# Transposing x by DMA on its way in, with a written issue order, in a one-core SwiGLU kernel

## The chip, the cores and the metric

The kernel runs on one core of one Trainium2 chip. The metric is device time in microseconds (us), median of several runs. The profile also gives a span, from the first to the last instruction; in every run listed with a span the time is about 1.8 us longer than the span. With one core there is no second core to compare with, so a run is called slow when it is over 1.5% above the fastest run of the same kernel, and fast otherwise.

Words used below: TensorE does the matmuls and writes them to PSUM (the tiles gate_ps, up_ps, o_ps and pT); VectorE and ScalarE do the elementwise work; SyncE's queue issues the DMA transfers, so a transfer has an issue (the queue is occupied; 0.44 us for the first load of x in the kernel before) and a landing (the data has arrived; 3.5 us after the start of that issue). The warm-up is a row of matmuls without use, run while the first data is on its way, meant to have TensorE's clock up when real work begins: in the kernel before the warm-up's matmuls run 427 ns apart, those of the steady stretches 216. In the profile lines PE is TensorE, PEld its weight loads, DVE VectorE, ACT ScalarE, POOL GpSimd and SPq SyncE's queue; PE, PEclk and DMA rows have one digit per fortieth of the span (a slice, counted from 0): busy tenths, or tenths of the full clock.

## The reference

```python
B, S, D, F = 32, 32, 512, 1792        # bf16; B*S = 1024 rows
gate = x @ w1                          # [1024, 512] x [512, 1792]
up   = x @ w3
h    = silu(gate) * up
out  = h @ w2                          # [1024, 1792] x [1792, 512]
```

In this kernel both operands of a matmul lie with the dimension that is summed over on the 128 partitions (the rows of on-chip memory), so the projections need x with its 512 columns on partitions, that is transposed.

## The kernel before

x is loaded as it lies (two loads of 512 KB), transposed on TensorE in 128x128 tiles through PSUM, and copied to `xT`. The Tile scheduler decides the order of each engine's instructions.

```python
nc.sync.dma_start(out=x_sb[:, 0:half, :], in_=x_view[:, 0:half, :])
for i, (cb0, cb1) in enumerate(bounds):            # chunks of 2, 2, 2, 4, 4 tiles of F
    nc.sync.dma_start(out=w1_sb[...], in_=w1_v[...])
    nc.sync.dma_start(out=w3_sb[...], in_=w3_v[...])
    if i == 3:
        nc.sync.dma_start(out=x_sb[:, half:NT, :], in_=x_view[:, half:NT, :])
# ... w2 in two halves, nine warm-up matmuls on a zeroed tile ...
def x_transposes(nb):
    for dt in range(DT):
        pT = psum_t.tile([P, NB], bf16, name="pT", tag="tp")
        for j in range(NT_PER_BLK):
            nt = nb * NT_PER_BLK + j
            nc.tensor.transpose(pT[:, j*P:(j+1)*P], x_sb[:, nt, dt*P:(dt+1)*P], ident[:])
        # copy pT to xT: VectorE for block 0, ScalarE for block 1
for nb in range(NBLK):                              # 2 blocks of 512 rows
    x_transposes(nb)
    for fo in range(FT):                            # 14 tiles of F
        # 4 gate matmuls, 4 up matmuls (128x512), sigmoid, two multiplies into hT
# then 8 tiles of out: 14 matmuls each over hT and w2, copy, store
```

Of the kernel before, what the change touches and what calls it, by code (L numbers as in the profile page):

```python
# [1 line left out]

# [5 lines left out]


@with_exitstack
def kernel(
    ctx: ExitStack,
    tc: tile.TileContext,
    x: bass.AP,
    w1: bass.AP,
    w3: bass.AP,
    w2: bass.AP,
    out: bass.AP,
):  # L20
    nc = tc.nc
    P = nc.NUM_PARTITIONS
    fp32 = mybir.dt.float32
    bf16 = mybir.dt.bfloat16

    B, S, D = x.shape
    F = w1.shape[1]
    N = B * S
    assert D % P == 0 and F % P == 0 and N % P == 0
    DT = D // P  # L30
    FT = F // P
    NT = N // P
    NB = 512
    assert N % NB == 0 and NB % P == 0
    NBLK = N // NB
    NT_PER_BLK = NB // P

    x_flat = x.flatten_outer_dims()
    out_flat = out.flatten_outer_dims()
    x_view = x_flat.rearrange("(nt p) d -> p nt d", p=P)  # L40
    w1_v = w1.rearrange("(dt p) f -> p dt f", p=P)
    w3_v = w3.rearrange("(dt p) f -> p dt f", p=P)
    w2_v = w2.rearrange("(ft p) d -> p ft d", p=P)

    consts = ctx.enter_context(tc.tile_pool(name="consts", bufs=1))
    work = ctx.enter_context(tc.tile_pool(name="work", bufs=3))
    psum_t = ctx.enter_context(tc.tile_pool(name="psum_t", bufs=2, space=bass.MemoryType.PSUM))
    psum = ctx.enter_context(tc.tile_pool(name="psum", bufs=2, space=bass.MemoryType.PSUM))
    psum2 = ctx.enter_context(tc.tile_pool(name="psum2", bufs=2, space=bass.MemoryType.PSUM))

    warm_sb = consts.tile([P, NB], bf16, name="warm_sb")
    nc.gpsimd.memset(warm_sb[:], 0.0)  # L52
    ident = consts.tile([P, P], bf16, name="ident")
    make_identity(nc, ident[:])

    x_sb = consts.tile([P, NT, D], bf16, name="x_sb")
    xT = consts.tile([P, DT, N], bf16, name="xT")
    w1_sb = consts.tile([P, DT, F], bf16, name="w1_sb")
    w3_sb = consts.tile([P, DT, F], bf16, name="w3_sb")
    w2_sb = consts.tile([P, FT, D], bf16, name="w2_sb")  # L60
    hT = consts.tile([P, FT, N], bf16, name="hT")

    half = NT // 2
    nc.sync.dma_start(out=x_sb[:, 0:half, :], in_=x_view[:, 0:half, :])  # L64

    chunk_sizes = [2, 2, 2, 4, 4]
    bounds = []
    cb = 0
    for csz in chunk_sizes:
        ce = min(FT, cb + csz)  # L70
        if cb < ce:
            bounds.append((cb, ce))
        cb = ce
    assert cb >= FT, (cb, FT)

    for i, (cb0, cb1) in enumerate(bounds):
        f0, f1 = cb0 * P, cb1 * P
        nc.sync.dma_start(out=w1_sb[:, :, f0:f1], in_=w1_v[:, :, f0:f1])  # L78
        nc.sync.dma_start(out=w3_sb[:, :, f0:f1], in_=w3_v[:, :, f0:f1])  # L79
        if i == 3:  # L80
            nc.sync.dma_start(out=x_sb[:, half:NT, :], in_=x_view[:, half:NT, :])

    FH = FT // 2
    nc.sync.dma_start(out=w2_sb[:, 0:FH, :], in_=w2_v[:, 0:FH, :])
    nc.sync.dma_start(out=w2_sb[:, FH:FT, :], in_=w2_v[:, FH:FT, :])

    NWARM = 9
    warm_ps = psum_t.tile([P, NB], fp32, name="warm_ps", tag="tp")
    for i in range(NWARM):
        nc.tensor.matmul(  # L90
            warm_ps[:],
            lhsT=warm_sb[:, 0:P],
            rhs=warm_sb[:],
            start=True,
            stop=True,
        )

    def x_transposes(nb: int):
        for dt in range(DT):
            pT = psum_t.tile([P, NB], bf16, name="pT", tag="tp")  # L100
            for j in range(NT_PER_BLK):
                nt = nb * NT_PER_BLK + j
                nc.tensor.transpose(  # L103
                    pT[:, j * P : (j + 1) * P],
                    x_sb[:, nt, dt * P : (dt + 1) * P],
                    ident[:],
                )
            if nb == 0:
                nc.vector.tensor_copy(xT[:, dt, nb * NB : (nb + 1) * NB], pT[:])  # L109
            else:  # L110
                nc.scalar.copy(xT[:, dt, nb * NB : (nb + 1) * NB], pT[:])  # L111

    for nb in range(NBLK):
        x_transposes(nb)
        for fo in range(FT):
            gate_ps = psum.tile([P, NB], fp32, name="gate_ps")
            up_ps = psum.tile([P, NB], fp32, name="up_ps")
            for dt in range(DT):
                nc.tensor.matmul(  # L119
                    gate_ps[:],  # L120
                    lhsT=w1_sb[:, dt, fo * P : (fo + 1) * P],
                    rhs=xT[:, dt, nb * NB : (nb + 1) * NB],
                    start=(dt == 0),
                    stop=(dt == DT - 1),
                )
            for dt in range(DT):
                nc.tensor.matmul(  # L127
                    up_ps[:],
                    lhsT=w3_sb[:, dt, fo * P : (fo + 1) * P],
                    rhs=xT[:, dt, nb * NB : (nb + 1) * NB],  # L130
                    start=(dt == 0),
                    stop=(dt == DT - 1),
                )
            sig = work.tile([P, NB], fp32, name="sig")
            nc.scalar.activation(  # L135
                sig[:], gate_ps[:], mybir.ActivationFunctionType.Sigmoid
            )
            t = work.tile([P, NB], fp32, name="t")
            nc.vector.tensor_mul(t[:], gate_ps[:], sig[:])  # L139
            nc.vector.tensor_mul(hT[:, fo, nb * NB : (nb + 1) * NB], t[:], up_ps[:])  # L140

    for nt in range(NT):
        DB = 256 if nt == NT - 1 else 512
        assert D % DB == 0
        for db in range(D // DB):
            o_ps = psum2.tile([P, DB], fp32, name="o_ps", tag="o_ps")
            for fo in range(FT):
                nc.tensor.matmul(  # L148
                    o_ps[:],
                    lhsT=hT[:, fo, nt * P : (nt + 1) * P],  # L150
                    rhs=w2_sb[:, fo, db * DB : (db + 1) * DB],
                    start=(fo == 0),
                    stop=(fo == FT - 1),
                )
            o_sb = work.tile([P, DB], bf16, name="o_sb", tag="o_sb")
            if nt == NT - 1:
                nc.vector.tensor_copy(o_sb[:], o_ps[:])  # L157
            else:
                nc.scalar.copy(o_sb[:], o_ps[:])  # L159
            nc.sync.dma_start(  # L160
                out=out_flat[nt * P : (nt + 1) * P, db * DB : (db + 1) * DB],
                in_=o_sb[:],
            )


# [1 line left out]
_INS = ['x', 'w1', 'w3', 'w2']  # L167
_OUTS = [((32, 32, 512), 'bfloat16')]


# [23 lines left out]
```

## Time and profile before

| | before |
|---|---|
| time, median (4 runs beside the changed kernel) | 93.24 us (93.17 to 93.61) |
| span of the profiled run (another run; with the 1.8 us, one of some 92.5) | 90.7 us |
| TensorE matmul busy | 82.4 us, 91% |
| granted TensorE clock, mean | 0.962 |

TensorE is the engine that sets the end, so one looks for holes in its row of slices and for stretches where its matmuls come slower than the usual 216 ns. The lines are in the prediction.

### The profile page before, as it was taken

How to read it: one execution, taken by the hardware profiler on the slowest of the kernel's cores; microseconds unless marked ns; L12 is line 12 of the kernel's file. 1: busy time of each engine (PE TensorE's matmuls, PEld its weight loads, DVE VectorE, ACT ScalarE, POOL GpSimd, SP SyncE). 2: the span in 40 equal slices, each digit the busy share in tenths (PEclk: the TensorE clock that was granted, in tenths of full speed). 3: DMA queues.
4: the chain of work that ended last, by engine and by line, in shares of the span. 5: the costliest groups of instructions: out<-in, count | busy, mean ns of one | idle time of the engine just before them, and what ended most of it. 6: DMA issues, size and time to landing. Idle time of an engine off the chain costs nothing.

```text
span 90.7 us, 1029 instructions
## 1 busy us (share of the span) xinstructions
PE 82.4 (91%) x391; PEld 38.4 (42%) x391; DVE 40.9 (45%) x62; ACT 24.2 (27%) x40; POOL 1.2 (1%) x7
## 2 busy tenths in 40 slices
PE   4999606999999999999999999999999999999960
PEld 1364202334444444544444444444444444444750
DVE  0045540336887887835887888788600000000030
ACT  5002200213234224385225224324122022202200
POOL 5000000000000000000000000000000000000000
PEclk9999995559999999999999999999999999999999
DMA  1999999996000000000000000000001110211021
GB/s 26 331 299 292 343 347 350 348 348 205 0 7 0 0 0 0 0 0 0 0 0 0 4 7 0 0 0 4 0 0 58 58 58 0 65 58 58 0 87 29
DMA packets 9461, 7.67 MB, mean 85 GB/s; under 512 B 368, under 2 KB 9456, under 8 KB 9456
## 3 DMA queue, kind: packets, MB, share of 16 engines
q1 hardware_dynamic: 9456, 7.60, 27.4%
q8 instruction: 3, 0.05, 0.2%
q14 instruction: 2, 0.02, 0.1%
HBM read 6.55 MB, written 1.05 MB: 84 GB/s over the span
## 4 chain that ended last, share of the span: by engine, by line
PE 81%; DMA 8%; SPq 6%; issue 1%; DVE 0%; DVEq 0%
PE gate_ps L119 27%; PE o_ps L148 27%; PE up_ps L127 26%; DMA x_sb<-in_x_dram 8%; SPq L79 3%; SPq L78 3%; PE pT L103 2%; SPq L64 0%; DVE o_sb L157 0%; DVEq L157 0%
## 5 line engine op out<-in xcount | busy, mean ns | idle before, releaser
L119 PE MATMUL gate_ps<-xT,w_sb 128*128 128x512 bf16 x112 | 31.3, 397 | 0.1
L127 PE MATMUL up_ps<-xT,w_sb 128*128 128x512 bf16 x112 | 29.9, 389 | 0.0
L135 ACT ACTIVATE sig<-gate_ps 128x512 f32<-128x512 f32 x28 | 16.7, 597 | 42.5 <-PE gate_ps L119 42.5
L139 DVE TENSOR_TENSOR t<-gate_ps,sig 128x512 f32<-128x512 f32 x28 | 19.4, 692 | 15.5 <-ACT sig L135 15.3
L148 PE MATMUL o_ps<-w_sb,hT 128*128 128x512 bf16 (+1 forms) x126 | 24.5, 355 | 0.0
L140 DVE TENSOR_TENSOR hT<-t,up_ps 128x512 bf16<-128x512 f32 x28 | 19.2, 687 | 3.8 <-PE up_ps L127 1.2
L127 PEld LDWEIGHTS <-w_sb 128*128 128x128 bf16 x112 | 11.3, 100 | 14.6 <-issue 2.5
L148 PEld LDWEIGHTS <-hT 128*128 128x128 bf16 x126 | 12.3, 98 | 11.9
L119 PEld LDWEIGHTS <-w_sb 128*128 128x128 bf16 x112 | 11.2, 101 | 13.3 <-issue 1.7
L157 DVE CAST o_sb<-o_ps 128x256 bf16<-128x256 f32 x2 | 0.9, 426 | 22.2 <-PE o_ps L148 22.2
L159 ACT CAST o_sb<-o_ps 128x512 bf16<-128x512 f32 x7 | 4.1, 585 | 17.5 <-PE o_ps L148 17.5
L103 PE MATMUL pT<-ident,x_sb 128*128 128x128 bf16 x32 | 3.5, 250 | 4.0 <-DMA x_sb<-in_x_dram 3.9
L103 PEld LDWEIGHTS <-x_sb 128*128 128x128 bf16 x32 | 2.8, 115 | 6.1 <-DMA x_sb<-in_x_dram 4.3
L90 PE MATMUL warm_ps<-warm_sb 128*128 128x512 bf16 x9 | 4.0, 631 | 1.3 <-POOL warm_sb L52 1.3
L109 DVE COPY xT<-pT 128x512 bf16<-128x512 bf16 x4 | 1.7, 425 | 5.9 <-PE pT L103 5.8
L90 PEld LDWEIGHTS <-warm_sb 128*128 128x128 bf16 x9 | 1.2, 142 | 3.2 <-issue 1.9
L111 ACT COPY xT<-pT 128x512 bf16<-128x512 bf16 x4 | 2.1, 587 | 0.4 <-PE pT L103 0.4
L135 ACT ACT_TABLE_LOAD x1 | 1.3, 1283 | 0.7 <-PEq L178 0.7
L52 POOL MEMSET warm_sb<- 128x512 bf16 x1 | 0.5, 524 | 0.3 <-POOLq L178 0.3
masks.py:199 POOL TENSOR_SCALAR_AFFINE_SELECT ident<-ident 128x128 bf16<-128x128 bf16 x1 | 0.3, 292 | 0.1
masks.py:197 POOL MEMSET ident<- 128x128 bf16 x1 | 0.2, 205 | 0.0
L178 POOL MEMSET const-float32-0.0<- 128x1 f32 x1 | 0.1, 98 | 0.2 <-issue 0.2
(3 smaller groups left out, 0.3 us busy)
## 6 DMA issues: line engine op xcount, KB each, us to landing
w_sb<-in_w_dram SPq DMA_DIRECT2D x4, 512.0 KB, 7.2
w_sb<-in_w_dram SPq DMA_DIRECT2D x2, 896.0 KB, 10.4
w_sb<-in_w_dram SPq DMA_DIRECT2D x6, 256.0 KB, 5.1
x_sb<-in_x_dram SPq DMA_DIRECT2D x2, 512.0 KB, 5.5
out_dram<-o_sb SPq DMA_DIRECT2D x7, 128.0 KB, 1.7
out_dram<-o_sb SPq DMA_DIRECT2D x2, 64.0 KB, 1.5
```

The source lines that it names most:

```text
L78: nc.sync.dma_start(out=w1_sb[:, :, f0:f1], in_=w1_v[:, :, f0:f1])
L79: nc.sync.dma_start(out=w3_sb[:, :, f0:f1], in_=w3_v[:, :, f0:f1])
L90: nc.tensor.matmul(warm_ps[:], lhsT=warm_sb[:, 0:P], rhs=warm_sb[:], start=True, stop=True,)
L103: nc.tensor.transpose(pT[:, j * P : (j + 1) * P], x_sb[:, nt, dt * P : (dt + 1) * P], ident[:],)
L111: nc.scalar.copy(xT[:, dt, nb * NB : (nb + 1) * NB], pT[:])
L119: nc.tensor.matmul(gate_ps[:], lhsT=w1_sb[:, dt, fo * P : (fo + 1) * P], rhs=xT[:, dt, nb * NB : (nb + 1) * NB], start=(dt == 0), stop=(dt ...
L127: nc.tensor.matmul(up_ps[:], lhsT=w3_sb[:, dt, fo * P : (fo + 1) * P], rhs=xT[:, dt, nb * NB : (nb + 1) * NB], start=(dt == 0), stop=(dt = ...
L135: nc.scalar.activation(sig[:], gate_ps[:], mybir.ActivationFunctionType.Sigmoid)
L139: nc.vector.tensor_mul(t[:], gate_ps[:], sig[:])
L140: nc.vector.tensor_mul(hT[:, fo, nb * NB : (nb + 1) * NB], t[:], up_ps[:])
L148: nc.tensor.matmul(o_ps[:], lhsT=hT[:, fo, nt * P : (nt + 1) * P], rhs=w2_sb[:, fo, db * DB : (db + 1) * DB], start=(fo == 0), stop=(fo == ...
L159: nc.scalar.copy(o_sb[:], o_ps[:])
```

## The change

The intent is to take the transposes off TensorE and the copies off VectorE and ScalarE, and to fix the order of instructions by hand. The core of the diff:

```diff
+    ctx.enter_context(tc.manual_schedule())
-    nc.sync.dma_start(out=x_sb[:, 0:half, :], in_=x_view[:, 0:half, :])
+    def load_x_transposed(n0, n1):
+        nc.sync.dma_start_transpose(out=xT[:, :, n0:n1], in_=x_flat[n0:n1, :])
...
+    load_x_transposed(0, HB)        # HB = 256 rows
+    load_w(0, 2)                    # w1 and w3, tiles 0 and 1
+    load_x_transposed(HB, NB)
+    load_w(2, 4)
+    load_w(4, 6)
+    load_x_transposed(NB, N)        # rows 512 to 1023
+    load_w(6, 10)
+    load_w(10, FT)
...
-            lhsT=warm_sb[:, 0:P],   # a tile zeroed by GpSimd
+            lhsT=one.to_broadcast([P, P]),
...
-    x_transposes(nb)                # 32 transposes and 8 copies in all
+    project(g0, w1_sb, 0, 0, HB, 0)     # the first two tiles in two halves of 256 rows:
+    project(g1, w1_sb, 1, 0, HB, 0)     # g0 g1 u0 u1 on the first, then on the second
...
```

PSUM is divided anew: three buffers each for gate and up in place of two.

More of the change, by code (lines that the diff above doesn't have):

```diff
@@ L5 @@
 import concourse.tile as tile
-from concourse import bass_utils, mybir
+from concourse import mybir
 from concourse._compat import with_exitstack
-from concourse.masks import make_identity
 @with_exitstack
@@ L24 @@
     bf16 = mybir.dt.bfloat16
+    SIGMOID = mybir.ActivationFunctionType.Sigmoid
     B, S, D = x.shape
@@ L28 @@
     N = B * S
-    assert D % P == 0 and F % P == 0 and N % P == 0
+    NB = 512
+    HB = NB // 2
     DT = D // P
@@ L32 @@
     NT = N // P
-    NB = 512
-    assert N % NB == 0 and NB % P == 0
     NBLK = N // NB
     NT_PER_BLK = NB // P
+    assert D % P == 0 and F % P == 0 and N % NB == 0
     x_flat = x.flatten_outer_dims()
     out_flat = out.flatten_outer_dims()
-    x_view = x_flat.rearrange("(nt p) d -> p nt d", p=P)
     w1_v = w1.rearrange("(dt p) f -> p dt f", p=P)
@@ L46 @@
     work = ctx.enter_context(tc.tile_pool(name="work", bufs=3))
-    psum_t = ctx.enter_context(tc.tile_pool(name="psum_t", bufs=2, space=bass.MemoryType.PSUM))
-    psum = ctx.enter_context(tc.tile_pool(name="psum", bufs=2, space=bass.MemoryType.PSUM))
-    psum2 = ctx.enter_context(tc.tile_pool(name="psum2", bufs=2, space=bass.MemoryType.PSUM))
-    warm_sb = consts.tile([P, NB], bf16, name="warm_sb")
-    nc.gpsimd.memset(warm_sb[:], 0.0)
-    ident = consts.tile([P, P], bf16, name="ident")
-    make_identity(nc, ident[:])
-    x_sb = consts.tile([P, NT, D], bf16, name="x_sb")
+    psum_o = ctx.enter_context(tc.tile_pool(name="psum_o", bufs=2, space=bass.MemoryType.PSUM))
+    psum = ctx.enter_context(tc.tile_pool(name="psum", bufs=3, space=bass.MemoryType.PSUM))
+    ctx.enter_context(tc.manual_schedule())
     xT = consts.tile([P, DT, N], bf16, name="xT")
@@ L61, with load_w1, load_w3, load_w @@
     hT = consts.tile([P, FT, N], bf16, name="hT")
-    half = NT // 2
-    nc.sync.dma_start(out=x_sb[:, 0:half, :], in_=x_view[:, 0:half, :])
-    chunk_sizes = [2, 2, 2, 4, 4]
-    bounds = []
-    cb = 0
-    for csz in chunk_sizes:
-        ce = min(FT, cb + csz)
-        if cb < ce:
-            bounds.append((cb, ce))
-        cb = ce
-    assert cb >= FT, (cb, FT)
-    for i, (cb0, cb1) in enumerate(bounds):
-        f0, f1 = cb0 * P, cb1 * P
-        nc.sync.dma_start(out=w1_sb[:, :, f0:f1], in_=w1_v[:, :, f0:f1])
-        nc.sync.dma_start(out=w3_sb[:, :, f0:f1], in_=w3_v[:, :, f0:f1])
-        if i == 3:
-            nc.sync.dma_start(out=x_sb[:, half:NT, :], in_=x_view[:, half:NT, :])
+    def load_x_transposed(n0, n1):
+        nc.sync.dma_start_transpose(out=xT[:, :, n0:n1], in_=x_flat[n0:n1, :])
+    def load_w1(c0, c1):
+        nc.sync.dma_start(out=w1_sb[:, :, c0 * P : c1 * P], in_=w1_v[:, :, c0 * P : c1 * P])
+    def load_w3(c0, c1):
+        nc.sync.dma_start(out=w3_sb[:, :, c0 * P : c1 * P], in_=w3_v[:, :, c0 * P : c1 * P])
+    def load_w(c0, c1):
+        load_w1(c0, c1)
+        load_w3(c0, c1)
+    load_x_transposed(0, HB)
[6 more added lines that the diff above has]
+    load_w(10, FT)
     FH = FT // 2
@@ L85 @@
     nc.sync.dma_start(out=w2_sb[:, FH:FT, :], in_=w2_v[:, FH:FT, :])
+    one = nc.const_aps.tensor(1.0, [P, 1], bf16)
+    warm_ps = psum_o.tile([P, NB], fp32, name="warm_ps", tag="o_ps")
     NWARM = 9
-    warm_ps = psum_t.tile([P, NB], fp32, name="warm_ps", tag="tp")
     for i in range(NWARM):
@@ L91 @@
             warm_ps[:],
-            lhsT=warm_sb[:, 0:P],
-            rhs=warm_sb[:],
+            lhsT=one.to_broadcast([P, P]),
+            rhs=one.to_broadcast([P, NB]),
             start=True,
@@ L96, with project @@
         )
-    def x_transposes(nb: int):
+    def project(ps, w_sb, fo, n0, n1, c0):
         for dt in range(DT):
-            pT = psum_t.tile([P, NB], bf16, name="pT", tag="tp")
-            for j in range(NT_PER_BLK):
-                nt = nb * NT_PER_BLK + j
-                nc.tensor.transpose(
-                    pT[:, j * P : (j + 1) * P],
-                    x_sb[:, nt, dt * P : (dt + 1) * P],
-                    ident[:],
-                )
-            if nb == 0:
-                nc.vector.tensor_copy(xT[:, dt, nb * NB : (nb + 1) * NB], pT[:])
-            else:
-                nc.scalar.copy(xT[:, dt, nb * NB : (nb + 1) * NB], pT[:])
@@ L113 @@
-    for nb in range(NBLK):
-        x_transposes(nb)
-        for fo in range(FT):
-            gate_ps = psum.tile([P, NB], fp32, name="gate_ps")
-            up_ps = psum.tile([P, NB], fp32, name="up_ps")
-            for dt in range(DT):
-                nc.tensor.matmul(
-                    gate_ps[:],
-                    lhsT=w1_sb[:, dt, fo * P : (fo + 1) * P],
-                    rhs=xT[:, dt, nb * NB : (nb + 1) * NB],
-                    start=(dt == 0),
-                    stop=(dt == DT - 1),
-                )
-            for dt in range(DT):
-                nc.tensor.matmul(
-                    up_ps[:],
-                    lhsT=w3_sb[:, dt, fo * P : (fo + 1) * P],
-                    rhs=xT[:, dt, nb * NB : (nb + 1) * NB],
-                    start=(dt == 0),
-                    stop=(dt == DT - 1),
-                )
-            sig = work.tile([P, NB], fp32, name="sig")
-            nc.scalar.activation(
-                sig[:], gate_ps[:], mybir.ActivationFunctionType.Sigmoid
-            )
-            t = work.tile([P, NB], fp32, name="t")
-            nc.vector.tensor_mul(t[:], gate_ps[:], sig[:])
-            nc.vector.tensor_mul(hT[:, fo, nb * NB : (nb + 1) * NB], t[:], up_ps[:])
@@ new lines, in project, with gate_up_tiles, swiglu @@
+            nc.tensor.matmul(
+                ps[:, c0 : c0 + n1 - n0],
+                lhsT=w_sb[:, dt, fo * P : (fo + 1) * P],
+                rhs=xT[:, dt, n0:n1],
+                start=(dt == 0),
+                stop=(dt == DT - 1),
+            )
+    def gate_up_tiles():
+        gate_ps = psum.tile([P, NB], fp32, name="gate_ps")
+        up_ps = psum.tile([P, NB], fp32, name="up_ps")
+        return gate_ps, up_ps
+    def swiglu(gate_ps, up_ps, fo, nb):
+        sig = work.tile([P, NB], fp32, name="sig")
+        nc.scalar.activation(sig[:], gate_ps[:], SIGMOID)
+        t = work.tile([P, NB], fp32, name="t")
+        nc.vector.tensor_mul(t[:], gate_ps[:], sig[:])
+        nc.vector.tensor_mul(hT[:, fo, nb * NB : (nb + 1) * NB], t[:], up_ps[:])
@@ new lines @@
+    g0, u0 = gate_up_tiles()
+    g1, u1 = gate_up_tiles()
+    project(g0, w1_sb, 0, 0, HB, 0)
+    project(g1, w1_sb, 1, 0, HB, 0)
+    project(u0, w3_sb, 0, 0, HB, 0)
+    project(u1, w3_sb, 1, 0, HB, 0)
+    project(g0, w1_sb, 0, HB, NB, HB)
+    project(g1, w1_sb, 1, HB, NB, HB)
+    project(u0, w3_sb, 0, HB, NB, HB)
+    project(u1, w3_sb, 1, HB, NB, HB)
+    swiglu(g0, u0, 0, 0)
+    swiglu(g1, u1, 1, 0)
+    for nb in range(NBLK):
+        for fo in range(2 if nb == 0 else 0, FT):
+            gate_ps, up_ps = gate_up_tiles()
+            project(gate_ps, w1_sb, fo, nb * NB, (nb + 1) * NB, 0)
+            project(up_ps, w3_sb, fo, nb * NB, (nb + 1) * NB, 0)
+            swiglu(gate_ps, up_ps, fo, nb)
@@ L142 @@
     for nt in range(NT):
-        DB = 256 if nt == NT - 1 else 512
-        assert D % DB == 0
+        DB = D // 2 if nt == NT - 1 else D
         for db in range(D // DB):
-            o_ps = psum2.tile([P, DB], fp32, name="o_ps", tag="o_ps")
+            o_ps = psum_o.tile([P, DB], fp32, name="o_ps", tag="o_ps")
             for fo in range(FT):
```

## The prediction

> **What bounds the kernel now.** I read the page's first two parts for the busy engine and the place of its holes, then the stretches between the holes, then the waits, and last the chain that ended last, to see what ends each hole.
>
> Busy shares and slices (2.27 us each) of the kernel before:
>
> ```profile
> PE 82.4 (91%) x391; PEld 38.4 (42%) x391; DVE 40.9 (45%) x62; ACT 24.2 (27%) x40; POOL 1.2 (1%) x7
> ...
> PE   4999606999999999999999999999999999999960
> ...
> PEclk9999995559999999999999999999999999999999
> DMA  1999999996000000000000000000001110211021
> GB/s 26 331 299 292 343 347 350 348 348 205 0 7 0 0 0 0 0 0 0 0 0 0 4 7 0 0 0 4 0 0 58 58 58 0 65 58 58 0 87 29
> ```
>
> TensorE carries the time. From slice 8 on it is full, but at slices 4 to 6 there is a hole, and after the hole the granted clock is 0.5 for three slices. The loads stream at some 340 GB/s to the end of slice 9 (about 22 us), so in the hole the DMA is the busy part.
>
> The stretches, with busy us and count for PE and PEld first, the granted clock later in the row:
>
> ```profile
> 5.10:10.70 5.60, 5.38 (x33) 2.85 (x31) 2.66 (x6) 1.19 (x2) 0.00 (x0) 1.00 1.15 317
> 10.70:14.50 3.80, 0.01 (x1) 0.02 (x2) 1.62 (x3) 0.00 (x0) 0.00 (x0) 0.83 1.10 347
> 14.50:18.60 4.10, 4.10 (x12) 1.58 (x13) 0.69 (x1) 0.60 (x1) 0.00 (x0) 0.50 1.10 349
> ...
> 38.20:41.50 3.30, 3.28 (x26) 1.71 (x24) 1.20 (x2) 2.50 (x5) 0.00 (x0) 1.00 0.00 0
> ```
>
> The second row is an idle TensorE, the third the same engine fully busy at half clock, the fourth the transposes of the second half of x between the two projection blocks. Who ended the idle time (the waits: us in total, times, longest):
>
> ```profile
> PE pT L103 <- DMA x_sb<-in_x_dram: 3.9, 1, 3.9
> ```
>
> One transpose of the SECOND half of x, which nothing needs before 38 us, was put by the scheduler into TensorE's in-order stream at 10.6 us, ahead of matmuls whose data was there. The chain, in order of time (start, us, what):
>
> ```profile
> 7.02 7.42 DMA x_sb<-in_x_dram
> 14.88 2.56 PE gate_ps L119 x6
> 17.44 1.71 PE up_ps L127 x4
> 19.15 0.85 PE gate_ps L119 x2
> 20.00 0.96 PE up_ps L127 x4
> 20.96 0.86 PE gate_ps L119 x4
> ...
> 63.97 23.79 PE o_ps L148 x124
> ```
>
> The second load of x is issued at 7.02 and lands at 14.44, behind 2.6 MB of weights. Then 6 matmuls take 2.56 us (427 ns each) where later 4 take 0.86 (216 ns each): that is the half clock, and it lasts to about 20.2.
>
> **The account of TensorE.** Needed at 216 ns per 128x512 matmul: 224 for gate and up, 48.4 us; 98 of o_ps, 21.2; 28 half-width ones at 0.109, 3.05 (96 x 0.216 + 28 x 0.109 = 23.79, the chain's last row). Sum 72.6 us. The first transpose starts at 5.12 and the last matmul ends at 87.76: 82.6 us. The 10.0 us over are:
> - 5.12 to 10.63: 5.51 us holding 16 matmuls (3.46): 2.05 for 16 transposes and their copies to xT.
> - 10.63 to 14.49: 3.86 idle.
> - 14.49 to 20.96: 6.47 us for 16 matmuls (3.46): 3.0, nearly all half clock, the rest two transposes.
> - 38.22 to 41.52: 3.30 us for 10 matmuls (2.16): 1.14 for 14 transposes.
> Before 5.12 lies the warm-up, after 87.76 a tail of 2.9 us (copy and store); 93.28 less the span of 90.7 leaves 2.6 that no engine shows. The last two stay.
>
> [...] an idle 3.86 us is followed by half clock, and nine warm-up matmuls from 1.31 on run 427 ns apart, with full speed by 5.12. But after the hole it took 5.7 us (14.49 to 20.2) to come back[...]. [...] here a record has a median of 219 ns, the copies are 425 ns on VectorE and 587 ns on ScalarE. [...]
>
> **The change part by part.**
> Removed: 32 transposes on TensorE, 8 copies, and with them the 2.05 and the 1.14 us. VectorE's and ScalarE's 1.7 and 2.1 us of copies lay beside TensorE and give nothing more.
> Written order: the instruction order of the changed kernel has no wait of block 0 on the last third of x; that load (rows 512 to 1023) is first read by block 1. So the 3.86 us hole and the 3.0 us half clock behind it go, unless a new hole arises.
> Warm-up: nine matmuls as before, but on a constant that exists before the start barrier, so they no longer wait 1.31 us for a memset; they can start at about 0.75 (SP's first issue is at 0.73). They end at 0.75 + 9 x 0.427 = 4.6.
> New: the first real matmul now waits for a transposed 256 KB of x and 256 KB of w1. First bytes in the kernel before: 26 GB/s in slice 0 is 0.06 MB, so at some 330 GB/s the stream starts at about 2.1; the first x (512 KB, 1.58 us at that rate) lands 3.5 us after issue, at 4.2, so landing lags the stream by some 0.55. [...]
> Needs of TensorE from 4.6 on: the first 16 half-width matmuls (0.11 us each) run to 6.36, the second 16 to 8.1; then 1.73 us per pair of gate and up: chunk 2 is wanted at 8.1, chunk 3 at 11.6, chunk 4 at 15.0, chunk 5 at 22, x's last half at 29. [...]
> PSUM: gate and up get three buffers each, and the path sigmoid 0.60, multiplies 0.69 + 0.69 fits beside 1.73; VectorE needs 1.38 per pair. No new wait there.
> Sum: start 4.6, work 72.6 + 0.1 for the split, ends 77.3; tail 2.9 gives a span of 80.2; plus 2.6 makes 82.8. The same from the other side: 93.28 - 10.0 - 0.5 (earlier start) = 82.8. I add 0.4 for a clock that may not yet be released at 4.6 (a matmul at half clock loses 0.21 us)[...]: 84.2.
>
> **The rivals.**
> Slow transposes. They share one in-order issue queue with the weights, so their time delays everything behind. At 170 GB/s (an estimate, half of the 340 seen for plain loads) x's first quarter takes 1.55 us, w1 lands at about 5.0, the second quarter of x at 7.3 against a need of 6.8, chunk 4 at about the need: 0.9 us lost, 83.7. At 100 GB/s: w1 at 6.0, a hole of 1.6 us before the second quarter and 1.2 before chunk 4: about 87. [...] For this: 256-byte pieces of x where the loads before had 1 to 2 KB at 340 GB/s[...]. Against: [...]that the split into quarters, with two gates and two ups interleaved, looks like the work of somebody who saw the first quarter arrive.
> Slow issue. SP needed 0.44 us to issue the first x and 0.50 for each 256 KB of weights. If a transposing issue takes 2 us, w1 lands about 1.5 us later: 84.5 to 85.5.
> The clock. [...] The trace's 5.7 us to recover speaks for taking it seriously.
> Loads hidden anyway. If the hole of 3.86 us had really been a lack of weights, removing the transpose would only move it. Against: the wait names x alone, and the chunks up to the sixth tile were issued by 3.4 us; by the stream rate (2.1 us plus 2.1 MB at 335 GB/s) they landed by about 9.
>
> **Range and chances.** The hole, the half clock and the transposes are 10 us that depend on nothing but order and removal; only slow transposes or a second clock dip can give much back. Low end 82.3 (no stall, clock released at once), high end 88.5 (transposes near 90 GB/s, or a clock dip). Faster by 2% means below 91.4: 0.90. Within 2% 0.06, slower 0.04[...].
>
> **What would show it.** Right: first gate matmul at 4.6 to 5.5, granted clock 1.0 from then on, matmuls 216 ns apart without a break to the output's first tile near 53, no PE wait on x over 1 us, span near 81 to 82. Wrong: TensorE waiting for xT on its first or second quarter, or for w_sb at the fourth chunk; GB/s in slices 1 to 4 far below 300; a transposing issue of over 1 us on SP; PEclk at 5 after slice 2.

The sum came to 84.2: 82.8, the 0.4 for the clock, and about 1.0 for slow transposes. The rates of 170, 100 and 90 GB/s are assumptions; the sums over the first two are estimates that add the 335 GB/s of the stream before. The "219 ns" is the median record of a 128x128 transpose on TensorE.

## The result, and the profile after

| | before | after |
|---|---|---|
| time, median | 93.24 us (93.17 to 93.61) | 83.75 us (83.23 to 84.88) |
| span of the profiled run | 90.7 us | 81.4 us |
| first transpose or gate matmul | 5.12 us | 5.75 us |
| last matmul ends | 87.76 us | 78.55 us |

One of the four runs after, 84.88, is slow. The ratio is 0.9121 (95% interval 0.9009 to 0.9233). Ratios are the mean time of one kernel's fast runs over that of the other's of the same rounds, so not quite the ratio of the medians quoted. The forecast was 84.2 with 82.3 to 88.5.

The page of the changed kernel, the busy row and the slices (2.04 us each) that answer to those shown of before:

```profile
PE 76.8 (94%) x375; PEld 36.8 (45%) x375; DVE 39.2 (48%) x58; ACT 22.0 (27%) x36; POOL 0.2 (0%) x4
...
PE   6959999999999999999999999999999999999950
...
PEclk9999999999999999999999999999999999999999
DMA  0799999999990000000000000000011101101111
GB/s 0 166 278 266 288 244 199 377 354 349 351 332 24 0 0 0 0 0 0 0 4 8 0 0 0 0 0 0 28 37 64 43 22 64 49 28 64 56 40 32
```

The hole at slices 4 to 6 is gone and no slice has a clock of 5. What is left is one slice at 5 near the start. Slices 1 to 6 of the GB/s row are lower, 166 to 288 where before had 292 to 350. Not all of that comes with transposing: plain x (below) moved 227 GB/s from 2 to 6 us, where the changed kernel moved 223; from 6 to 10 us it was 307 against 271, from 10 to 14 us 347 against 216. The 166 of slice 1 is partly a stream with little issued yet (DMA busy 7 tenths); the next lowest, 199, is at the end of the third transposing load (issued at 7.17, landed at 13.1). The loads last into slice 12 (some 24.5 us).

The changed kernel's chain, in order of time (start, us, what):

```profile
0.73 1.31 SPq L57
2.10 3.60 DMA w_sb<-in_w_dram
5.75 1.05 PE gate_ps L95 x8
6.79 0.87 PE up_ps L95 x8
...
54.33 24.22 PE o_ps L140 x126
```

The first row is the ISSUE of the first transposing load on SyncE. Only after it, at 2.10, is w1 issued; it lands at 5.70, and the first gate matmul starts. From there TensorE runs to the end with hardly a break: 5.75 to 78.55 is 72.8 us, against the 72.6 of pure work. Its only recorded wait for data (us in total, times, longest):

```profile
PE gate_ps L95 <- DMA w_sb<-in_w_dram: 1.0, 1, 1.0
```

So of the span's 9.3 us, the account of the prediction gives 10.05 back (2.05 + 3.86 + 3.0 + 1.14), less 0.63 for the later start (5.75 against 5.12) and 0.17 lost in the first gate matmuls; the tail after the last matmul is 2.85, as before.

### The profile page after: what moved, and what is told of

Same layout as the page of the kernel before. It is cut to its first block, busy times and chain, and to the rows that moved or that the text cites. A ratio compares the mean times of both kernels' runs of the same rounds, so it can differ in the third digit from the quotient of the medians.

```text
span 81.4 us, 984 instructions
## 1 busy us (share of the span) xinstructions
PE 76.8 (94%) x375; PEld 36.8 (45%) x375; DVE 39.2 (48%) x58; ACT 22.0 (27%) x36; POOL 0.2 (0%) x4
## 2 busy tenths in 40 slices
DMA packets 12597, 7.67 MB, mean 94 GB/s; under 512 B 4528, under 2 KB 12592, under 8 KB 12592
## 3 DMA queue, kind: packets, MB, share of 16 engines
HBM read 5.51 MB, written 1.05 MB: 80 GB/s over the span
## 4 chain that ended last, share of the span: by engine, by line
PE 89%; DMA 4%; SPq 2%; DVE 1%; issue 0%; DVEq 0%
PE gate_ps L95 30%; PE o_ps L140 30%; PE up_ps L95 30%; DMA w_sb<-in_w_dram 4%; SPq L57 2%; DVE o_sb L149 1%; DVEq L149 0%
## 5 line engine op out<-in xcount | busy, mean ns | idle before, releaser
L95 PEld LDWEIGHTS <-w_sb 128*128 128x128 bf16 x240 | 23.3, 98 | 26.7 <-DMA w_sb<-in_w_dram 2.2
L95 PE MATMUL gate_ps<-xT,w_sb 128*128 128x512 bf16 (+1 forms) x120 | 28.8, 365 | 1.0 <-DMA w_sb<-in_w_dram 1.0
L95 PE MATMUL up_ps<-xT,w_sb 128*128 128x512 bf16 (+1 forms) x120 | 28.8, 365 | 0.0
L85 PE MATMUL warm_ps<-const-bfloat16-1.0 128*128 128x512 bf16 x9 | 4.0, 626 | 0.8 <-PEq L170 0.8
L85 PEld LDWEIGHTS <-const-bfloat16-1.0 128*128 128x128 bf16 x9 | 1.2, 138 | 2.7 <-issue 2.7
```

The source lines that it names most:

```text
L85: nc.tensor.matmul(warm_ps[:], lhsT=one.to_broadcast([P, P]), rhs=one.to_broadcast([P, NB]), start=True, stop=True,)
L95: nc.tensor.matmul(ps[:, c0 : c0 + n1 - n0], lhsT=w_sb[:, dt, fo * P : (fo + 1) * P], rhs=xT[:, dt, n0:n1], start=(dt == 0), stop=(dt == D ...
```

## The experiments

The open question was which part of the change bought the time: the order, or the removal of the transposes; and what sets the new start. Eleven kernels were run (on chips 8, 1 and 1); the kernel before had medians of 92.61, 92.37 and 92.42 us (91.14 to 94.40 over all, its fast runs 91.14 to 92.72).

| kernel | order | transposes | median us | all runs | fast runs |
|---|---|---|---|---|---|
| before | scheduler | TensorE | 92.4 to 93.2 | 91.14 to 94.40 | 91.14 to 92.72 in these calls |
| order-only | written | TensorE | 84.98 | 84.82 to 85.31 | all 4 |
| half by DMA | written | block 0 TensorE, block 1 DMA | 84.39 | 84.14 to 84.66 | all 6 |
| DMA, scheduled | scheduler | DMA | 83.87 | 83.27 to 85.11 | 83.27 to 83.92 (5 of 7) |
| changed (again) | written | DMA | 84.82 | 83.47 to 85.62 | 83.47 to 84.32 (3 of 6) |

The other parts of the change (warm-up on a constant, the first tiles in halves, three PSUM buffers) were not tested apart.

**Order only.**

```diff
 # the kernel before
+    ctx.enter_context(tc.manual_schedule())
...
-        x_transposes(nb)
+        if nb == 0:
+            x_transposes(0, range(DT))
         for fo in range(FT):
+            if nb == 0 and 8 <= fo < 12:
+                x_transposes(1, [fo - 8])
```

> The kernel before with a written issue order and nothing else: x loaded plainly, transposed on TensorE and copied, the second half's transposes written four at a time ahead of tiles 8 to 11 of block 0. My account: the hole of 3.86 us and the half clock behind it (2.6) go, block 0's 2.05 stays, block 1's 16 transposes cost about 1.0 in place of 1.5 (1.14 and the two early ones): 86.3 to 86.8 us. Rival (the hole was really late weights and comes back elsewhere): TensorE waits for w_sb around 10 to 14 us and the time stays above 90.

Measured: 84.98 us, even less than the 86.3 expected; ratio 0.9226 (0.9159 to 0.9294). Some 0.6 us of the miss is that before itself ran at 92.61, and some 0.6 that block 0's transposes cost about 1.5 us (the first gate matmul at 6.50 after the first transpose at 5.05) where the account had 2.05. The written order alone, with every transpose still on TensorE, brings most of the gain (7.7% of some 9%). The timeline of this kernel shows what a group of four transposes costs when its data has long been there:

```profile
20.34 0.39 PE L105 MATMUL pT<-ident,x_sb 128*128 128x128 bf16 x4
20.57 1.03 PE L124 MATMUL gate_ps<-xT,w_sb 128*128 128x512 bf16 x4
```

The next matmul starts 0.23 us after the first transpose of the group: the 16 transposes of block 1 are 0.9 us of TensorE. No TensorE wait on weights came in the hole's place, so that rival falls.

**x early.** Is it really the one load?

```diff
 # the kernel before
-        if i == 3:
+        if i == 0:
             nc.sync.dma_start(out=x_sb[:, half:NT, :], in_=x_view[:, half:NT, :])
```

> The kernel before with one character changed: the load of the second half of x is issued after the first chunk of weights instead of after the fourth. TensorE's order is unchanged, so the early transposes stay where they are. If the hole is the wait for that load and nothing else, x's second half lands near 7.3 us, before TensorE asks at 10.6, the hole (3.86) and the half clock behind it (2.6) go: about 86.3 us, granted clock 1.0 throughout. If it is order as such that cost, or late weights: TensorE waits for w_sb instead and 90 us or more remain.

Measured: 85.90 us (85.13 to 86.40), ratio 0.9356 (0.9276 to 0.9435). One character takes about 6 us off (6.5 between the medians, 5.9 between the means of the fast runs). Its timeline shows the misplaced transposes where they were, no longer waiting, and in a second view the slice rows show neither hole nor half clock:

```profile
9.55 1.03 PE L127 MATMUL up_ps<-xT,w_sb 128*128 128x512 bf16 x4
10.41 0.28 PE L103 MATMUL pT<-ident,x_sb 128*128 128x128 bf16 x2
10.52 0.81 PE L119 MATMUL gate_ps<-xT,w_sb 128*128 128x512 bf16 x3
```

```profile
PE   3999999999999999999999999999999999999950
...
PEclk9999999999999999999999999999999999999999
```

**DMA, scheduled.** The changed kernel without the line `ctx.enter_context(tc.manual_schedule())`.

> The changed kernel without its written order: the scheduler orders the instructions, x is still transposed by three DMAs. It is the fourth corner beside before, order-only and the changed kernel. If the hole came only from transposes that the scheduler could put wrongly: with none in the stream the time is that of the changed kernel, 83.3 to 84.0 in fast runs. If written order is worth something of itself: a TensorE wait appears that the changed kernel has not, and it is slower by more than 0.5 us.

Measured: fast runs 83.27 to 83.92, two of seven runs near 85. That is the changed kernel's time. The two halves of the change are therefore in the main substitutes, not summands: once no transposes are in TensorE's stream there is nothing for the scheduler to misplace, and once the order is right the transposes cost little (order-only's 84.98 against 83.87).

**Half by DMA.** The order-only kernel with

```diff
-            nc.sync.dma_start(out=x_sb[:, half:NT, :], in_=x_view[:, half:NT, :])
+            nc.sync.dma_start_transpose(out=xT[:, :, NB:N], in_=x_flat[NB:N, :])
...
-                x_transposes(1, [fo - 8])
```

> The order-only kernel with the second half of x, alone, transposed by DMA; the first half stays on TensorE. It takes 16 transposes and 4 copies out of block 0. If each part costs what TensorE's account says, the gain over order-only (84.98) is 16 x 0.06 = 1.0 us: 84.0, with a spread under 0.6 us, since TensorE is never idle after its start. If the transposing load delays the last chunks of weights: TensorE waits for w_sb near 15 us and there is no gain.

Measured: 84.39 (84.14 to 84.66), against 84.98 of order-only on another chip: some 0.6 of the 1.0 us. Its spread is small, as expected. The profiles settle the rest: the first gate matmul came at 6.64 where order-only's has 6.50, and from there to the end of the last matmul are 72.75 us against 73.64. That is 0.89 less, near the 0.92 of four groups of transposes at 0.23.

**First weights on the other queue.** What sets the start at 5.75?

```diff
 # the changed kernel
-    load_w(0, 2)
+    load_w(0, 2, nc.scalar)
```

> Only the first chunk of w1 and w3 is issued from ScalarE's queue, beside the transposing load on SyncE's. Theory A (the start of the projections at 5.75 is set by the ISSUE of the transposing load, 1.31 us on SyncE, which pushes the issue of w1 to 2.10): w1 is issued at about 0.75 and lands by about 4, the first gate matmul starts right after the warm-up at 4.6 to 4.8, and the time falls by about 1.0 us, to about 82.7. Theory B (the start is set by the transposed data or by the DMA engines being slow in transposing): x's first quarter or w1 still lands near 5.5, and the time stays at 83.5 or more.

Measured: fast runs 83.55 to 83.67, no gain; three of six runs were slow. The chain of this kernel has another first link:

```profile
0.73 5.44 DMA xT<-in_x_dram
6.21 1.03 PE gate_ps L95 x8
```

With the weights out early, the first transposing load took 5.44 us to land where it took 3.1 alone, and the start moved back, to 6.21. So theory A, that the issue time alone sets the start, falls: the first link here is the landing of x. In flight beside it were w1, w3 and the second transposing load, issued right behind the first; which of them delayed it was not separated. Behind w1 alone (w1 first, below) the same load landed in 3.5 us.

**Plain x.** Wrong results: loads of the same size with nothing transposed.

```diff
-        nc.sync.dma_start_transpose(out=xT[:, :, n0:n1], in_=x_flat[n0:n1, :])
+        src = x_flat[n0:n1, :].rearrange("(p q) d -> p (q d)", p=P)
+        q = (n1 - n0) * D // P // DT
+        nc.sync.dma_start(out=xT[:, :, n0:n1], in_=src.rearrange("p (c q) -> p c q", q=q))
```

> Wrong results on purpose: the three loads of x are plain copies of the same size into the same tile, nothing is transposed anywhere. It takes away the whole cost of transposing by DMA. Theory A: the plain issue takes about 0.45 us instead of 1.31, w1 goes out at about 1.2, lands at 4.7 to 4.9, gate starts then; 82.5 us. The two later transposes cost nothing even now, so no more is gained. Theory B': the transposes also cost later, by slowing chunks of weights; then the gain is over 1.5 us.

Measured: 83.53 (82.75 to 83.78), where fast runs of the changed kernel in the same call were 83.47, 83.57 and 84.32. Neither theory's size was right. SyncE's issues in this kernel (start, us), and from its waits the longest of a matmul:

```profile
0.73 0.63 SPq L59 DMA_DIRECT2D xT<-in_x_dram  x1
1.42 0.60 SPq L62 DMA_DIRECT2D w_sb<-in_w_dram  x1
2.06 0.50 SPq L65 DMA_DIRECT2D w_sb<-in_w_dram  x1
```

```profile
PE up_ps L97 <- DMA w_sb<-in_w_dram: 1.1, 1, 1.1
```

The issue of x takes 0.63 us instead of 1.31 and the first gate starts at 4.85, as theory A has it, but then the up matmuls wait for w3 until 7.01. What the early start won was handed back. So with transposes made free the time fell by some 0.4 us (83.4, the mean of its runs, against 83.8 of those three), which so few runs hardly tell from nothing. It is no upper bound: had w3 come on time, up to the 1.1 us of its wait might have been gained as well, which no run shows. Why w3 took 4.90 us to land in this run (its stream ran at 204 and 209 GB/s from 4 to 6 us) stays open.

What the transposes cost the DMA engines is seen by comparing these two pages, of the changed kernel and then of plain x:

```profile
DMA packets 12597, 7.67 MB, mean 94 GB/s; under 512 B 4528, under 2 KB 12592, under 8 KB 12592
```

```profile
DMA packets 9989, 7.67 MB, mean 94 GB/s; under 512 B 384, under 2 KB 9984, under 8 KB 9984
```

The changed kernel has 4,144 more packets under 512 B. The trace of its profile has 4,096 of exactly 256 bytes, which make the 1.05 MB of x; that of the kernel before has none. In the stretch from 22 to 26 us the changed kernel's DMA was busy for a share of 0.67 and plain x's for 0.19: its loads ended some 1.9 us later. Part of that is not transposing: from 3.37 to 4.00 nothing was being transposed and its DMA was busy for a share of only 0.41. The rate itself can be read from the trace, whose 256-byte packets are the transposing loads. In the changed kernel those of the first load run from 2.10 to 3.37, alone, at 209 GB/s, and those of the third from 10.33 to 12.63, with few others, at 245, where the plain loads of the kernel before moved 347 to 349 from 10.7 to 18.6 us. It is no constant: in the unaltered kernel's second profile (below) the first load ran at 169 (2.12 to 3.81; 142 from 2 to 3 us, 178 from 3 to 4). The pages' HBM reads are 5.51 MB for the changed kernel and 6.55 for the kernel before, 1.04 MB less, the size of x, though 7.67 MB moved in both: as far as these pages show, what transposing loads read is not counted there.

**Again, and 13 warm-up matmuls.** The changed kernel unaltered, and with `NWARM = 13` in place of 9.

> The changed kernel once more, unaltered, to have its spread beside the runs of this call and a second profile. Expected 83.2 to 84.0 us, first gate matmul at 5.7 to 6.3, no stretch of half clock after the warm-up.

> The changed kernel with 13 warm-up matmuls instead of 9. Theory C (its spread from 83.5 to 85.6 is the clock: TensorE idles from 4.77 to 5.7 or 6.3, and in some runs the first 16 matmuls then run at half clock, 1.7 us): with no idle gap, all runs end at 83.3 to 84.2 and none above 84.5. Theory D (the spread comes from when the DMA lands x and w1): the spread of 2 us stays.

Measured: the unaltered kernel 83.47, 83.57, 84.32, and three slow runs at 85.32 to 85.62, so the expectation of no half clock failed; with 13 warm-up matmuls all six runs from 83.22 to 84.10. The profile of the unaltered kernel fell on a slow run here, and its chain shows what that is:

```profile
6.28 1.89 PE gate_ps L95 x8
8.17 1.71 PE up_ps L95 x8
9.88 1.01 PE gate_ps L95 x8
10.89 0.87 PE up_ps L95 x8
```

The first 16 half-width matmuls run at half rate (1.71 us for 8 in place of 0.87), after an idle 1.52 us between the warm-up's end and the first gate. The profiles of DMA scheduled and x last, slow runs too, show the same 1.89 and 1.71 us; the other slow runs were not profiled. The page's clock row reads 9 all through, so the rate of the matmuls has to be read, not that row (it reads 1.00 too from 1.3 to 5.1 us of before, with warm-up matmuls 427 ns apart). With 13 the idle time is filled, and the first gates run at full rate (start, us; the timeline of that kernel):

```profile
0.77 4.91 PE L85 MATMUL warm_ps<-const-bfloat16-1.0 128*128 128x512 bf16 x13 [0.77 <-PEq L170]
5.78 1.05 PE L95 MATMUL gate_ps<-xT,w_sb 128*128 128x256 bf16 x8
```

Theory C holds, as far as these runs go. Of 29 runs of the four kernels that idle 1 to 1.5 us there (the changed one, DMA scheduled, x last, first weights on the other queue), 11 took 84.88 us or more; of the 18 runs of the three without that idle time (this one and the two with w1 first), none took over 84.2. Plain x, with two gaps of 0.6 and 1.1 us, is in neither group: none of its six runs was slow. The fast runs are not moved by the longer warm-up. What the gap does to the clock is not shown: in the fast profile of the changed kernel too the nine warm-up matmuls ran at half rate to their end (4.00 us, as in the slow one), but its first gates, after a gap of 0.98 us, took 1.05 us for 8, so there the rate rose in the gap; in the slow one, 1.89 for 8 after 1.52 us, it had not.

**x last.** The third transposing load is first read near 30 us.

```diff
-    load_x_transposed(NB, N)        # after load_w(4, 6)
...
+    load_x_transposed(NB, N)        # after w2
```

> The changed kernel with the third transposing load (rows 512 to 1023, first read by block 1 near 30 us) moved behind w2. Its issue (4.0 us) and its slow transfer then delay no weights. Hidden theory: the fourth chunk of w3 lands by about 14 instead of 17.2, just ahead of its need, and since TensorE hardly waits there the time stays within 0.3 us of the changed kernel's fast runs (83.2 to 84.0). If the delay of the weights costs: 0.5 us or more faster.

Measured: fast runs 83.08 to 83.94, two slow ones at 84.90 and 85.05. No difference that these runs can tell: the transfer of x's second half (5.9 us from issue to landing in the changed kernel, 11.3 here) is hidden, though the move did bring the issue of the fourth chunk of w3 forward, to 7.89 from 11.84. It is not hidden by much. With 13 warm-up matmuls the chain ran through it:

```profile
6.97 4.51 SPq L57
12.15 5.25 DMA w_sb<-in_w_dram
17.45 1.04 PE up_ps L95 x4
```

There the third transposing issue held SyncE from 6.97 to 11.48, the fourth chunk of w3 landed at 17.40, and TensorE had waited 0.2 us for it.

**w1 first, and both.** In the second kernel the third transposing load is moved as well, to just ahead of w2.

```diff
+    load_w1(0, 2)
     load_x_transposed(0, HB)
-    load_w(0, 2)
+    load_w3(0, 2)
```

> The changed kernel with the first chunk of w1 issued ahead of the first transposing load, and w3 between the two. If the issue of the transposing load (1.31 us) in front of w1 sets the start: w1 goes out at 0.73, the transposing load at 1.25 and lands 3.1 to 3.6 later, the first gate matmul starts at 4.6 to 5.0 instead of 5.75 to 6.28, fast runs near 82.6. If the transposing load slows with any traffic beside it (it took 5.4 us to land beside w1 from the other queue): start near 6, no gain.

> Both: first chunk of w1 ahead of the first transposing load, and the third transposing load behind the last chunk of w1 and w3. The first gate starts at 4.8 as in the kernel with w1 first, the waits of 0.27 and 0.24 us on w_sb that it had near 9.7 and 17.9 shrink to one of them: 83.2 to 83.5, and what remains over 82.7 is half clock in the first 8 gate matmuls, as in that kernel (1.84 us for what takes 1.05 at full clock).

Measured: w1 first 83.70 (83.56 to 84.16), no gain where 82.6 was expected; both 83.37 (83.03 to 83.48), ratio 0.9046 (0.8999 to 0.9093). The start did move to 4.8 us, but in the first kernel's profile, which is of its slowest run, the matmuls did not reach full rate until 5.7 us after the first warm-up matmul (0.77 to 6.48):

```profile
4.82 1.84 PE L96 MATMUL gate_ps<-xT,w_sb 128*128 128x256 bf16 x8
6.48 1.06 PE L96 MATMUL up_ps<-xT,w_sb 128*128 128x256 bf16 x8
```

In the second kernel's profile they had it at once, with the gates 1.04 us from 4.80, but the ups then started only at 5.96. The last kernel is the best of all here: its six runs lie below the changed kernel's median, within 0.45 us, though its fastest is only 0.2 us ahead of the changed kernel's fastest. It was run at another time.

## Why the prediction was right, and where its terms were off

- **The account of 10.0 us was right.** Hole, half clock and transposes all went, and nothing took their place: TensorE works for 72.8 us without a break. That the hole was one load's late landing, as the prediction read from the wait, is shown by the kernel with x early. The experiments add what it did not see: DMA transposes without the order get all of the gain, the order alone 7.7% of some 9%.
- **The start was mis-sized: 4.6 forecast, 5.75 measured.** The step that failed is the estimate of the landings, which had x's first quarter and w1 there before the warm-up's end. x's first quarter landed at about 3.8 (0.73 + 3.1), but w1 at 5.70. That estimate gave the transposing issue no more time than a plain one; it took 1.31 us, and the first gate started at 4.85 in plain x, whose issue takes 0.63, and at 4.82 with w1 issued ahead. The rival "slow issue" had named this, and the size: 84.5 to 85.5 for a 2 us issue.
- **The constant was mis-sized: 2.6 us for what no engine shows, 1.8 measured.** 93.28 was the median, and the span of 90.7 that of another run; in every run listed with a span the time is about 1.8 us longer than the span: a run of before with a span of 90.8 took 92.61. This error of 0.8 us and the start's 1.15 nearly cancel: 82.8 + 1.15 - 0.8 + 0.1 (72.8 us of TensorE for 72.7) is 83.2, the profiled run. That the sum came so near is in this part luck.
- **The allowance of 0.4 for the clock was somewhat low as a mean and wrong as a shape:** nothing in most runs, about 1.7 us in the slow ones, if the 8 unprofiled are like the 3 profiled (11 of 29, which makes 0.6). The reading behind it, "with full speed by 5.12", is wrong: eight transposes of before from 5.12 on still took 314 ns each, the next eight mostly 219 (`--tile pT` of before in the windows 5.1:5.9 and 6.42:8; number, ns min/median/max, first and last start):

```profile
L103 PE MATMUL pT<-ident,x_sb x8: 314/314/314, 5.1 to 5.9; 128*128 128x128 bf16 x8
L103 PE MATMUL pT<-ident,x_sb x8: 219/219/264, 6.3 to 6.9; 128*128 128x128 bf16 x8
```

So in that profile the clock rose 4.6 to 5.0 us after the first warm-up matmul, where the reading has 3.8 at most, and a warm-up of 0.75 to 4.6 could not be counted on to have raised it. The time was no constant: in plain x the nine warm-up matmuls took 3.47 us in place of the changed kernel's 4.00, so the rate rose before their end, and in w1 first it took 5.7, as it did from the end of before's hole. Some 0.4 of the 2.05 us put down to transposes was this half clock (8 transposes 107 ns apart in place of 56).

- **The 1.0 us for slow transposes was not needed.** They ran at 209 and 245 GB/s for the first and third load of the profiled run, and with 13 warm-up matmuls the fourth chunk of w3 landed at 17.40, but TensorE needed it just then and waited no more than 0.2 us.
- **Four smaller readings were off, without effect on the sum.** The plain transfers came in pieces of 512 bytes and 1 KB (3,328 and 5,760 packets in the trace, stores included), not of 1 to 2 KB. Of the six loads of 256 KB only the first four took 0.50 us to issue (0.50 to 0.51), the others 0.93 and 1.06. Of the chunks up to the sixth tile the last was issued at 4.39, not by 3.4; they landed at 9.0 and 9.9, still before the transpose asked at 10.6. And TensorE is full from slice 7 on, though at half clock at first.

## What to carry to other kernels

When an engine that works in order waits for data that it needs much later (here 3.86 us, with matmuls behind whose data was there), look first for a misplaced instruction or a late load: one moved load here was worth about 70% of a rewrite (6.4% of some 9%). Moving transposes to the DMA is then worth what they cost on TensorE when nothing waits, here 0.23 us for four in midstream, plus the freedom that nothing can be misplaced. Keep the engine busy from the warm-up to the first real matmul, since with a gap of 1 to 1.5 us there 11 of 29 runs lost over a microsecond, and without it none of 18.
